# DeltaNet into a gated MLP on one core: the first three fetches of w_in issued from two queues instead of one

## The chip, the cores and the metric

One NeuronCore of a Trainium2 chip runs the whole program. The metric is the device time of one execution in microseconds (us); the time before is the median of 12 runs. The engines are TensorE (PE, with its weight loads PEld), VectorE (DVE), ScalarE (ACT), GpSimd (POOL) and SyncE (SP). SP, ACT and POOL also issue DMAs, each on a queue of its own: q1 is SP's, q10 is ACT's and q0 is POOL's. Sixteen DMA engines carry the packets of all three queues.

## The reference

```python
# attention: batch 4, heads 8, seq 768, head_dim 48, float32
k_n = k / (np.linalg.norm(k, axis=-1, keepdims=True) + 1e-06)
for t in range(S):
    y[:, :, t] = np.einsum('bhd,bhde->bhe', q[:, :, t], state)
    v_old = np.einsum('bhde,bhd->bhe', state, kt)
    state = state + bt[:, :, :, None] * np.einsum('bhd,bhe->bhde', kt, vt - v_old)
# heads joined: x is (3072, 384); w_in is (384, 2048), w_out is (2048, 384), both float64
h = x @ w_in
g = h * (1.0 / (1.0 + np.exp(-1.702 * h)))
return (g @ w_out).astype(np.float32)
```

## The kernel before

**The work.** The sequence is cut into 6 chunks of 128 steps. A unit is one chunk of one batch, so there are 24 units, each with 8 heads. For a unit the kernel normalizes the keys (`normalize_first` for the first seven tiles), transposes them (`transposed`), makes the Gram matrix `G` (`prepare`), sends it through DRAM (`Nd`) to gather the 32x32 diagonal blocks of all heads into `NT`, inverts those blocks on VectorE (`invert`), sends the inverses back through DRAM (`Yd`, then `XB`) and solves the chunk block by block on TensorE (`Step.solve`, `Step.below`) with ScalarE copies (`US`) and VectorE subtractions (`V`) between. The chunk's output goes through the MLP (`hidden`, `written`), whose matmuls fill TensorE for most of the span.

**The weights.** Both weight matrices are float64, and the kernel reads them as raw words. `fetch` brings a part of them into a stage, which lies in a piece of the tile `w_out` that is not yet used. `from_double` turns the two words of each number into float32 with six VectorE instructions (lines 182 to 194), or five and one of ScalarE (line 187) for parts other than the first three. A part of w_in is 128 partitions of 512 numbers. The first three fetches take three parts each (`together_with`): fetch 1 brings parts 0 to 2, fetch 2 parts 3 to 5, fetch 3 parts 6 to 8. Fetch 3 uses the same stage as fetch 1. Later parts are fetched by POOL.

**The four transfers of a fetch.** The rows of w_in are not in the order of the partitions, so a fetch of w_in is four DMAs, listed in `x_rows`: partitions 0 to 47, 48 to 63, 64 to 111 and 112 to 127. For three parts these carry 576, 192, 576 and 192 KB. Every packet is a row of 4096 bytes.

**Order.** The setup at the end of the kernel function issues things in this order: the keys of four units, fetch 1 (`ahead(1, sync)`), the conversion of its parts, the transposes and Gram matrices, the queries and values, more keys (tiles KN4 to KN6), fetches 2 and 3 (`ahead(2, sync)`, line 899), the inversion of the first four units (`invert(0)`), the normalization of KN4 to KN6, and then part 3 (`weights(W1)`). `pinned` operations keep their order in the program; the others are placed by the scheduler, which works from estimated times. The conversion of part 3 and the beginning of part 4 are not pinned. Each engine runs its list strictly in order, its DMA issues included, and a waiting instruction holds all that stand behind it. The line of most helpers is 105, so the names of the tiles tell the operations apart.

Of the kernel before, what the change touches and what calls it, by code (L numbers as in the profile page):

```python
# [18 lines left out]
def kernel(  # L19
# [19 lines left out]
    nc = tc.nc  # L39
# [7 lines left out]
    DP = 64  # L47
# [55 lines left out]
    def pinned(op):  # L103

        return lambda *a, **kw: tc.keep_in_program_order(op(*a, **kw))  # L105
# [106 lines left out]
    def stage(part):  # L212

        if part < parts_in:
            at = part % (2 * KC) * 2 * N_IN
            return at, at + 2 * N_IN
        f = part - parts_in
        if f >= FC - 2:
            return None
        depth = 2 if f < 2 or f >= 8 else 4  # L220
        if f >= 12:
            depth = 1
        at = FC * DM // (2 if f < 2 else 1) - (f % depth + 1) * 2 * DM
        return at, at + 2 * DM

    def together_with(part):

        return list(range(part, part + (KC if part < 3 * KC else 1)))
# [5 lines left out]
    def fetch(part, dma):  # L234

        if part < parts_in:
            j, f0 = part % KC, part // KC * N_IN
            parts = together_with(part)
            shape, src = (len(parts), N_IN), moe_w_in[:, f0 : f0 + N_IN]
            dst = w_in[:, j : j + len(parts), f0 : f0 + N_IN]  # L240
        else:
            parts = [part]
            shape, src = (1, DM), moe_w_out
            dst = target(part)
        if src.dtype != F32:
            if (s := stage(part)) is None:
                raw = wk.tile([128, *shape, 2], I32, tag="xT", name="raw", bufs=3)
            else:
                words = slice(s[0], stage(parts[-1])[1])
                raw = w_out.rearrange("p f d -> p (f d)")[:, words].bitcast(I32)  # L250
                raw = raw.rearrange("p (j n o) -> p j n o", j=shape[0], o=2)
            for i, p in enumerate(parts):
                stages[p] = raw[:, i]
                if s is not None:
                    taken[p] = stage(p)
            dst = raw.bitcast(src.dtype).rearrange("p j n o -> p j (n o)")
        if part < parts_in:
            for p, r, m, step in x_rows:
                row = src[r + j * step : r + j * step + m]
                dma(  # L260
                    out=dst[p : p + m],
                    in_=bass.AP(
                        row.tensor, row.offset, [row.ap[0], [row.ap[0][0] * step, len(parts)], row.ap[1]]
                    ),
                )
        else:
            r = (part - parts_in) * 128
            dma(out=dst if src.dtype == F32 else dst[:, 0], in_=src[r : r + 128, :])
        return parts

    def target(part):
        if part < parts_in:
            j, f0 = part % KC, part // KC * N_IN
            return w_in[:, j, f0 : f0 + N_IN]
        return w_out[:, part - parts_in, :]
# [394 lines left out]
    def ahead(n, dma=nc.gpsimd.dma_start):  # L670

        while n > 0 and waiting and free(waiting[0]):
            staged.extend(fetch(waiting.pop(0), dma))
            n -= 1
# [192 lines left out]
        follow(n)  # L867

    queue = []
    sync = pinned(nc.sync.dma_start)  # L870
    for b in range(0, B, HB):
        normalize_first(b)
    for i in range(B):
# [64 lines left out]
```

## Time and profile before

| | |
|---|---|
| median of 12 runs | 827.59 us (823.05 to 831.54) |
| the profiled execution: time, span | 829.96 us, 828.2 us |
| PE busy in the span | 773.8 us (93%) |
| PE busy from 31 to 57 us / from 220 to 828 us | 9.40 of 26 us / 599.92 of 608 us |
| DVE busy from 31 to 57 us / from 57 to 72 us | 24.48 of 26 us / 14.21 of 15 us |
| mean granted clock of TensorE | 0.946 |
| w_in transfers issued by SP | 6 of 576 KB and 6 of 192 KB |

Times of instructions are counted from the start of the span. A timeline row has the start, the length, the engine, the line, the operation, out<-in with shapes, the count, and in brackets the idle time of the engine before it with what ended that. A "q" behind an engine's name marks its sequencer, which issues DMAs.

### The profile page before, as it was taken

The numbers are of one execution on the slowest core, as the hardware profiler recorded it, in microseconds if no ns is written. First come the engines' busy times: TensorE is split into PE (matmuls) and PEld (weight loads), VectorE is DVE, ScalarE is ACT, GpSimd is POOL, SyncE is SP. The second block draws the span as 40 slices with busy tenths as digits, with TensorE's granted clock in tenths as the row PEclk, the third lists the DMA queues.
The fourth block names the chain that finished last, engine by engine and source line by source line (L and its number), as shares of the span: only waits on it lengthen the run. The fifth ranks groups of instructions, "written<-read, shape, count | busy, mean of one in ns | idle before, by whom it ended". The sixth has DMA issues, their size and how long they took to land.

```text
span 828.2 us, 18734 instructions
## 1 busy us (share of the span) xinstructions
PE 773.8 (93%) x8100; PEld 582.7 (70%) x8100; DVE 485.7 (59%) x1037; ACT 230.3 (28%) x499; POOL 132.0 (16%) x138
## 2 busy tenths in 40 slices
PE   8438798979979999999999999999999999999998
PEld 6327697646866776876867867867867768677684
DVE  6898888687876565675666667667656640100000
ACT  2303542232322332322332322322322323212120
POOL 2113120232021221221222123122201000000000
PEclk9659778987969999999999999999999999999999
DMA  9995732632123323223214204214212010000000
GB/s 146 201 165 138 184 84 66 145 95 76 46 42 81 72 52 78 45 62 85 62 26 101 62 21 101 53 28 94 52 48 56 11 41 11 11 16 1 24 1 19
DMA packets 147314, 55.96 MB, mean 68 GB/s; under 512 B 114336, under 2 KB 143232, under 8 KB 147232
## 3 DMA queue, kind: packets, MB, share of 16 engines
q1 hardware_dynamic: 139488, 41.96, 24.6%
q0 software_dynamic: 2752, 10.62, 4.5%
q10 hardware_dynamic: 4992, 2.20, 1.0%
q8 instruction: 63, 1.03, 0.5%
q14 instruction: 19, 0.16, 0.1%
HBM read 33.13 MB, written 20.45 MB: 65 GB/s over the span
## 4 chain that ended last, share of the span: by engine, by line
PE 75%; DVE 11%; issue 7%; DMA 4%; POOL 1%; ACT 1%; SPq 0%; DVEq 0%; POOLq 0%; ACTq 0%
PE po L105 28%; PE ph L105 25%; PE psY L105 5%; PE psU L105 4%; PE psQ L105 3%; PE ph L638 3%; DVE P L105 2%; PE psG L105 2%; DMA w_out<-in_moe_w_out_dram 2%; DVE YB L105 2%; PE psR L105 2%; PE psT L105 1%; DVE z L105 1%; DMA KN<-in_k_dram 1%; DVE w_in L105 1%
## 5 line engine op out<-in xcount | busy, mean ns | idle before, releaser
L105 PE MATMUL po<-w_out,gT 128*128 128x384 f32 x704 | 239.3, 490 | 0.0
L105 PE MATMUL ph<-xT,w_in 128*128 128x256 f32 x966 | 222.1, 384 | 0.3
L105 PEld LDWEIGHTS ph<-xT,w_in 128*128 128x128 f32 x966 | 180.4, 191 | 30.9 <-issue 2.3
L105 PEld LDWEIGHTS po<-w_out,gT 128*128 128x128 f32 x704 | 130.1, 190 | 82.6 <-issue 1.9
L105 DVE TENSOR_TENSOR V<-V,psR 64x384 f32<-64x384 f32 (+1 forms) x80 | 44.5, 556 | 193.1 <-PE psR L105 192.3
L105 DVE TENSOR_TENSOR P<-NT,YB 64x18 f32<-64x18 f32 (+25 forms) x171 | 82.7, 483 | 4.5
L105 ACT ACTIVATE gT<-ph 128x512 f32<-128x512 f32 x81 | 48.1, 594 | 116.0 <-PE ph L105 115.9
L105 DVE TENSOR_REDUCE YB<-P 64x6 f32<-64x18 f32 (+25 forms) x171 | 72.7, 425 | 5.5
L105 ACT COPY US<-psU 32x384 f32<-32x384 f32 x80 | 37.5, 469 | 123.7 <-PE psR L105 116.9
L105 PEld LDWEIGHTS psU<-V,XB 32*32 32x32 f32 x1280 | 46.0, 106 | 30.2 <-issue 21.2
L533 POOL TENSOR_SCALAR_AFFINE_SELECT M<-M 128x1024 f32<-128x1024 f32 x24 | 29.8, 1243 | 231.6 <-DVE M L105 162.4
L105 PE MATMUL psU<-V,XB 32*32 32x48 f32 x1280 | 54.5, 204 | 4.4 <-DVE V L105 3.9
L638 PE MATMUL ph<-xT,w_in 128*128 128x128 f32 (+1 forms) x282 | 52.1, 345 | 3.1 <-DMA xT<-last 3.1
L105 PE MATMUL psR<-US,G 32*32 32x48 f32 x1920 | 52.8, 203 | 0.3 <-ACT US L105 0.3
L638 PEld LDWEIGHTS ph<-xT,w_in 128*128 128x128 f32 x282 | 44.8, 218 | 7.8 <-issue 4.3
L105 PEld LDWEIGHTS psR<-US,G 32*32 32x32 f32 x1920 | 44.7, 105 | 1.0 <-issue 0.5
L313 POOL TENSOR_TENSOR rn<-ssq,half 128x8 f32<-128x8 f32 x17 | 38.9, 2290 | 2.9 <-DVE ssq L311 2.9
L90 POOL DMA_DIRECT2D KN<-in_k_dram x14 | 13.4, 955 | 154.0 <-PE psY L105 102.1
L154 PE MATMUL ps_warm<-ident 128*128 128x256 bf16 x152 | 21.5, 306 | 16.0 <-DVE ps_warm L105 13.7
L105 ACT COPY o<-po 128x384 f32<-128x384 f32 x22 | 10.5, 478 | 77.7 <-PE po L105 55.8
L105 DVE TENSOR_TENSOR P<-NT 64x256 f32<-64x256 f32 (+7 forms) x36 | 30.6, 849 | 0.3
L154 PEld LDWEIGHTS <-ident 128*128 128x128 bf16 x152 | 16.4, 109 | 19.8 <-issue 13.9
(144 smaller groups left out, 872.6 us busy)
## 6 DMA issues: line engine op xcount, KB each, us to landing
Nd<-G SPq DMA_DIRECT2D x20, 512.0 KB, 3.5
w_out<-in_moe_w_out_dram POOLq DMA_DIRECT2D x14, 384.0 KB, 3.8
QP<-in_q_dram SPq DMA_DIRECT2D x24, 192.0 KB, 3.9
V<-in_v_dram SPq DMA_DIRECT2D x24, 192.0 KB, 3.3
out_dram<-o SPq DMA_DIRECT2D x24, 192.0 KB, 1.9
w_out<-in_moe_w_in_dram SPq DMA_DIRECT2D x6, 576.0 KB, 12.2
NT<-Nd SPq DMA_DIRECT2D x24, 128.0 KB, 2.7
Yd<-YS SPq DMA_DIRECT2D x24, 128.0 KB, 3.2
```

What stands on the lines that cost most here:

```text
L90: dma(out=dst[n % len(dst)][:, :, 0:D], in_=src[b, :, c * C : (c + 1) * C, :].rearrange("h p d -> p h d"),)
L105: return lambda *a, **kw: tc.keep_in_program_order(op(*a, **kw))
L154: pe.matmul(ps, lhsT=ones[:, 0:128], rhs=ones, start=True, stop=True)
L313: nc.gpsimd.tensor_tensor(rn, ssq, half, op=ALU.pow)
L533: nc.gpsimd.affine_select(out=self.M, in_=self.M, compare_op=ALU.is_gt, fill=0.0, base=0, pattern=[[0, H], [1, 128]], channel_multiplier=-1,)
L638: pe.matmul(ph[:, u], lhsT=w_in[:, j, f * 128 : (f + 1) * 128], rhs=xT[:, j, t], start=(j == 0), stop=(j == KC - 1),)
```

## The change

In `fetch`, when the issuing function is SP's pinned one (`sync`), the DMAs for partitions 64 and up go to ACT's queue through a second pinned function (`beside`). This holds for fetches 1, 2 and 3 alike: six of their twelve DMAs move from SP to ACT. Fetches by POOL are not touched, and neither are sizes, stages or conversions.

```diff
         if part < parts_in:
             for p, r, m, step in x_rows:
                 row = src[r + j * step : r + j * step + m]
-                dma(
+                (beside if dma is sync and p >= DP else dma)(
                     out=dst[p : p + m],
...
     queue = []
-    sync = pinned(nc.sync.dma_start)
+    sync, beside = pinned(nc.sync.dma_start), pinned(nc.scalar.dma_start)
```

The built programs differ in three engines' lists; those of PE and POOL are the same. SP loses six DMA issues. ACT gains two of them before the first key transpose's copy, and four between the last of its copies into `M` (line 530) and its copy `NT<-YB` (line 436). On VectorE the conversions of parts 3 and 4 move: in the kernel before they stand in one piece behind the normalization of KN4 to KN6; in the changed one the two line-182 instructions stand inside the inversion, behind its last `TENSOR_REDUCE NT<-P`, two of line 193 among the four pairs of `P<-NT` and `YB<-P` after it, and two each of lines 191, 192 and 194 in the normalization.

## The prediction

> **What bounds the kernel now.** I read the windows by stage first. From 220 us on TensorE is busy 599.92 of 608 us. Before 72 us it is VectorE that works without a break:
>
> ```profile
> core 0: us, PE busy (x) PEld busy (x) DVE busy (x) ACT busy (x) POOL busy (x), PEclk, DMA share, GB/s
> ...
> 31.00:57.00 26.00, 9.40 (x60) 7.59 (x61) 24.48 (x47) 6.26 (x16) 4.36 (x3) 0.50 1.22 168
> 57.00:72.00 15.00, 14.05 (x158) 11.34 (x157) 14.21 (x36) 1.69 (x3) 3.27 (x6) 0.88 0.74 146
> ```
>
> Most of PE's 14.05 us there is `ps_warm` filler, whose result nobody uses. Everything that follows waits for the setup, so a microsecond lost on VectorE before 72 us is a microsecond at the end. The fetches of w_in also stand in this setup. VectorE's timeline shows where they touch it:
>
> ```profile
> 18.67 0.43 DVE L105 TENSOR_SCALAR w_in<-w_out 128x512 int32<-128x512 int32 x1 [1.76 <-DMA w_out<-in_moe_w_in_dram]
> ...
> 29.02 0.69 DVE L105 SCALAR_TENSOR_TENSOR w_in<-tmp,w_in 128x512 f32<-128x512 f32 x1
> 30.76 1.22 DVE L105 TENSOR_TENSOR NT<-NT,bI 128x1024 f32<-128x1024 f32 x1 [1.05 <-DMA NT<-Nd]
> ...
> 50.04 0.42 DVE L105 TENSOR_REDUCE NT<-P 128x64 f32<-128x256 f32 x1
> 50.56 0.42 DVE L105 TENSOR_TENSOR P<-NT 128x256 f32<-128x256 f32 x1
> ...
> 66.01 0.76 DVE L182 TENSOR_SCALAR w_in<-w_out 128x512 int32<-128x512 int32 x2
> ...
> 71.57 1.14 DVE L105 TENSOR_TENSOR V<-V,psR 32x384 f32<-32x384 f32 x2
> ```
>
> Fetch 1 holds VectorE up by 1.76 us, but its conversions end at 29.7 and VectorE then waits 1.05 us more, for `NT`, which comes through ScalarE's copies and DRAM and not from w_in. From 30.76 to 71.57 no idle time is marked. In particular nothing waits for fetch 2: its first conversion, line 182, stands at 66.01. Last, the queues: when they issue, when fetch 2 lands, and at what rate.
>
> ```profile
> 39.20 5.93 SPq L105 DMA_DIRECT2D w_out<-in_moe_w_in_dram  x8
> ```
>
> ```profile
> 43.48 0.65 ACT L530 COPY M<-psQ 128x256 f32<-128x256 f32 x2 [0.21 <-PE psQ L520]
> 44.07 0.64 ACT L436 ACTIVATE NT<-YB 128x256 f32<-128x256 f32 x1
> ```
>
> ```profile
> w_out<-in_moe_w_in_dram SPq DMA_DIRECT2D x1, 192.0 KB, 13.4
> ```
>
> ```profile
> GB/s 163 252 182 144 209 150 135 107 143 150 150 185 228 214 150 107 100 157 164 164 199 214 164 164 107 128 128 157 207 228 185 157 121 114 143 192 264 299 192 50
> ```
>
> The row with 13.4 is fetch 2's fourth transfer: issued at 41.34, landed 13.4 us later, at 54.7. Its second one, issued at 40.39 with 9.3 us, landed at 49.7. So a half (576 + 192 KB, 0.786 MB) takes 5.0 us on one queue, 157 GB/s. The last row is 41 to 64 us in forty slices of 0.575 us. Inside a half the rate sinks to 100 to 128; where one half ends and the next begins, and the 16 engines work on both, it rises to 199 to 228.
>
> **Fetch 1, part by part.** SP loses two issues of 0.31 and 0.43 us behind which it only waits for `Nd`: worth nothing. ACT gets two; their semaphores came at 5.64 us at the latest, and ACT's next work is at 13.53: hidden. If the two halves share the engines well the fetch lands earlier, at best taking away the 1.76 us; the wait for `NT` then grows by as much, so the gain is 0. If it lands later, 1.05 us is covered. One thing is at risk: the keys of the fourth unit, on SP's queue until 8.36 (issued 2.72, 5.64 us), would share the engines with ACT's words. VectorE reads them at 11.71, so 3.3 us cover them; if ACT's half went wholly ahead (5.0 us) 1.7 us would be lost. I take 0, because few key packets are left when ACT's first words can flow.
>
> **Fetch 2, the term that counts.** The program order of the changed kernel puts both line-182 instructions directly behind the reduce of 50.04, so at 50.46 us, and they wait for all four transfers. ACT can issue its two only after its `M` copies: the last of these starts near 43.8, since ACT's list is strict. They then are not alone: SP's queue has gone on to the lower half of fetch 3, so the two queues share the engines, packet by packet. Reckoned from landings: issue 43.8, plus 2.7 us for a short transfer (the page's median of the 128 KB `NT<-Nd`), gives 46.5; then 0.786 MB at half of the joint rate R.
>
> - Lower end of R: one queue's 157 GB/s. 10.0 us, landed at 56.5, a wait of 6.0 us.
> - Upper end: two full queues, 314. 5.0 us, landed at 51.5, a wait of 1.0 us.
> - Taken: 214, the mean of the seven seam slices (209, 228, 214, 199, 214, 207, 228), the only rows in which engines work on different halves. 7.35 us, landed at 53.85, a wait of 3.4 us.
>
> So the words land about when they did before (54.7), but the instruction that wants them has moved from 66.0 to 50.5.
>
> A rule of the Trainium skill speaks against the change: SBUF — State Buffer, section "Can I just issue two DMAs to hit both halves?", says that two concurrent DMAs on tiles at partitions 0 and 64 were measured at only 6% over one, because they serialize on the same engines. The seam slices contradict it in part, since they run 36% over the mean of a half. By the page R would be 166 GB/s, the landing 56.0 and the sum below 5.8 instead of 3.7; I follow the slices.
>
> **What moves on VectorE.** The conversions are the same instructions with the same durations, so `V` at 71.57 comes later by the wait alone. But 0.67 us of line 182 and 1.2 us of line 193 now stand before the memset that releases the 66 `ps_warm` matmuls (57.11 to 66.23). After that filler `psU` comes 1.87 later, at 68.10 instead of 66.74, since 0.51 of it was a wait for `XB`. That is 1.36 us; the first `psR` ended at 69.83 and `V` began at 71.57, so it is covered with 0.4 us to spare. The next filler carries it on: `psU` at 73.04 instead of 72.17, and the second `psR`, which ACT's `US` released at 74.95 while PE was free at 74.38, begins at 75.25. That costs 0.3 us (between 0 and 0.87). `XB` itself lands in time: its transfers come 1.9 us and the wait later, but no longer queue behind fetch 3.
>
> **ScalarE.** Four issues of 0.44 us now stand ahead of `NT<-YB`, which would start near 45.6 instead of 44.07; even at 1.7 us each, the longest issue of these transfers, it ends at 51.3. The reader is the `P<-NT` of 50.56, which itself is held by the wait; without the wait this cover would be 5 us at 0.44 and gone at 1.7. The matmuls' lists and POOL's are unchanged, so what follows shifts as a whole.
>
> **Sum.** 0 (fetch 1) + 3.4 (wait for fetch 2) + 0.3 (filler) = 3.7 us. On the profiled execution, 829.96 us for a span of 828.2, that makes 833.7. This execution is 2.4 us above the median of 827.59, so on the median it is 831.3, 0.45% more. 0.3% is 2.5 us, about what a measurement of this kernel can tell from no change.
>
> **Rivals.**
>
> - *The halves do not mix* (R at 157 to 166). For it: the DMA share is already full. Against it: the seams. Wait 5.5 to 6.0, plus 0.3: 833.4 to 833.9.
> - *The halves do not hinder each other* (R near 314, or ACT's issues start earlier), so not slower. The wait is 0 to 1.0 us and decides from a landing at 51.5 or before: 827.9 to 828.9. For it: at 62 us, when few packets are left, slices reach 264 and 299. Against: no slice between 42 and 60 us passes 228.
> - *The keys are late.* ACT's words overtake the fourth key tile, up to 1.7 us on top: 833.0.
> - *The clock turns it faster.* The granted clock was 0.80 from 72 to 110 us and 0.88 from 110 to 220. Another pattern of load in the setup could raise the second: 100.19 us busy, so 0.03 more is worth 3.4 us, which from about the middle estimate on cancels the wait: 827.9, or 824.5 if the wait is absent too. It could as well fall. No row says which.
>
> **How the numbers follow.** The mixed case gets 0.47, its own range 829.8 to 832.8 (R from 185 to 260). No mixing gets 0.17, no hindrance 0.20, late keys 0.06, the clock 0.10. Slower by over 0.3% (above 830.1): most of the mixed case, no mixing and late keys, 0.62. Faster by over 0.3% (below 825.1): the clock with the wait absent, and what I have not seen, 0.11. Within: 0.27. The range that leaves out 2 in 10 runs from no hindrance, less 1.4 us for the scatter of the runs, to no mixing with 1.6 us of scatter: 826.5 to 835.5.
>
> **What would show it.** Right: VectorE idle by 2 to 5 us before line 182, near 50.5 us, put down to the DMA of w_in; the fourth transfer of fetch 2 landing at 52.5 to 55.5; `V` near 75 us; the wait before the first conversion smaller or gone, that before `NT` larger, and `NT` itself still at 30.8. Wrong: line 182 without a wait, or `NT` not at 30.8. Slices steady at 214 or more over 45 to 58 us show the mixing; 157 shows the rival.

## The result, and the profile after

The changed kernel takes 834.41 us (median of 12 runs, 829.89 to 839.0), the kernel before beside it 826.96 (median of 49). The ratio is 1.0081, with a 95% interval of 1.0059 to 1.0104: by the ratio 6.7 us slower (4.9 to 8.6); the two medians differ by 7.45. The profiled execution took 832.58 us, its span was 830.8 us and its mean granted clock 0.947.

VectorE's timeline of the changed kernel, at the places shown of before:

```profile
19.02 0.43 DVE L105 TENSOR_SCALAR w_in<-w_out 128x512 int32<-128x512 int32 x1 [2.22 <-DMA w_out<-in_moe_w_in_dram]
...
30.88 1.22 DVE L105 TENSOR_TENSOR NT<-NT,bI 128x1024 f32<-128x1024 f32 x1 [0.82 <-DMA NT<-Nd]
...
50.22 0.42 DVE L105 TENSOR_REDUCE NT<-P 128x64 f32<-128x256 f32 x1
60.64 0.76 DVE L182 TENSOR_SCALAR w_in<-w_out 128x512 int32<-128x512 int32 x2 [10.00 <-DMA w_out<-in_moe_w_in_dram]
...
81.32 1.14 DVE L105 TENSOR_TENSOR V<-V,psR 32x384 f32<-32x384 f32 x2 [1.12 <-PE psR L105]
```

Up to the reduce near 50 us none of these rows has moved by more than 0.35 us. Then line 182, which stood at 66.01, is next in the list, and VectorE stands still for 10.00 us until the words of fetch 2 are there. `V` begins 9.75 us later than before. The windows show the same hole: VectorE's 14.21 busy us from 57 to 72 us have become 11.29, and from 31 to 57 us 24.48 have become 18.37.

```profile
31.00:57.00 26.00, 9.41 (x60) 7.59 (x61) 18.37 (x39) 6.33 (x16) 4.13 (x3) 0.50 1.21 170
57.00:72.00 15.00, 3.18 (x16) 2.19 (x16) 11.29 (x19) 1.33 (x2) 0.00 (x0) 0.50 0.41 67
```

The issues: SyncE's four transfers (the lower halves of fetches 2 and 3), then ScalarE's four (the upper halves), in the timelines of their sequencers, and ScalarE's next work.

```profile
39.47 3.32 SPq L105 DMA_DIRECT2D w_out<-in_moe_w_in_dram  x4
```

```profile
43.89 0.34 ACTq L105 DMA_DIRECT2D w_out<-in_moe_w_in_dram  x1
...
44.27 1.42 ACTq L105 DMA_DIRECT2D w_out<-in_moe_w_in_dram  x3
45.81 0.66 ACT L436 ACTIVATE NT<-YB 128x256 f32<-128x256 f32 x1 [1.32 <-DVE P L105]
```

The list of DMA issues has the time to landing; its second row answers to the 13.4 of before.

```profile
w_out<-in_moe_w_in_dram ACTq DMA_DIRECT2D x3, 576.0 KB, 14.5
...
w_out<-in_moe_w_in_dram ACTq DMA_DIRECT2D x3, 192.0 KB, 16.2
```

Both medians are those of fetch 2's upper half, issued at 43.89 and 44.27 us: landed at 58.43 and 60.45. Before, the last of fetch 2 had landed at 54.75.

Why so late is told by the queues of the DMA engines in three windows, each with packets, MB and share of 16 engines: 44 to 50 us, 50 to 53 us, 54 to 62 us.

```profile
q1 hardware_dynamic: 246, 0.87, 104.1%
```

```profile
q1 hardware_dynamic: 98, 0.30, 68.1%
q10 hardware_dynamic: 44, 0.18, 33.3%
```

```profile
q10 hardware_dynamic: 334, 1.15, 97.5%
q1 hardware_dynamic: 2, 0.00, 0.3%
```

In the first window SyncE's queue q1 has the engines for itself, though ScalarE's transfers had been issued before 46 us. Packets of ScalarE's queue q10 begin at 50.6 us, where those of q1 run out, the lower half of fetch 3 included; that half landed at 53.97 and 56.65. The profile does not tell which engine moved a packet: that each engine goes over when it is done with q1 is inferred from the middle window, in which both queues move packets. Nor did the transfer rate rise. The slices of 41 to 64 us, as shown of before:

```profile
GB/s 167 204 202 178 214 207 128 150 135 157 157 135 150 114 142 135 199 135 121 171 185 235 207 164 171 128 164 142 142 157 142 121 178 150 121 107 71 50 7 0
```

All twelve transfers are in at 64.14, against 63.69 before.

### The profile page after: what moved, and what is told of

The parts are those of the page before. It is cut to its first block, busy times and chain, and to the rows that moved or that the text cites. A ratio compares the mean times of both kernels' runs of the same rounds, so it can differ in the third digit from the quotient of the medians.

```text
span 830.8 us, 18734 instructions
## 1 busy us (share of the span) xinstructions
PE 769.4 (93%) x8100; PEld 578.3 (70%) x8100; DVE 484.7 (58%) x1037; ACT 230.7 (28%) x499; POOL 130.8 (16%) x138
## 4 chain that ended last, share of the span: by engine, by line
PE 81%; DMA 6%; issue 6%; DVE 5%; POOL 1%; ACT 1%; SPq 0%; POOLq 0%; DVEq 0%; ACTq 0%
PE po L105 28%; PE ph L105 24%; PE psY L105 5%; PE psU L105 4%; PE psQ L105 3%; DMA w_out<-in_moe_w_in_dram 3%; PE ps_warm L154 2%; PE ph L638 2%; PE psG L105 2%; DMA w_out<-in_moe_w_out_dram 2%; PE psR L105 2%; PE psT L105 1%; PE psG L367 1%; PE po L655 1%; DVE P L105 1%
## 5 line engine op out<-in xcount | busy, mean ns | idle before, releaser
L105 PEld LDWEIGHTS ph<-xT,w_in 128*128 128x128 f32 x966 | 180.0, 190 | 30.7 <-issue 2.3
L638 PE MATMUL ph<-xT,w_in 128*128 128x128 f32 (+1 forms) x282 | 47.7, 325 | 1.0 <-DMA xT<-last 1.0
L638 PEld LDWEIGHTS ph<-xT,w_in 128*128 128x128 f32 x282 | 41.0, 201 | 5.2 <-PE psT L352 1.2
L90 POOL DMA_DIRECT2D KN<-in_k_dram x14 | 13.4, 955 | 152.7 <-PE psY L105 102.1
```

Source lines behind the costliest of these rows:

```text
L90: dma(out=dst[n % len(dst)][:, :, 0:D], in_=src[b, :, c * C : (c + 1) * C, :].rearrange("h p d -> p h d"),)
L638: pe.matmul(ph[:, u], lhsT=w_in[:, j, f * 128 : (f + 1) * 128], rhs=xT[:, j, t], start=(j == 0), stop=(j == KC - 1),)
```

## The experiments

The theory after the result: the loss is one wait, made of a place (the conversion stands near 50 instead of 66 us) and of a landing (60.45 us), and the landing follows from an order of service, in which transfers of two queues are served by time of issue. Rivals: the second queue costs something by itself; SyncE's queue has priority; the queues share the engines, but slowly.

**Late conversions.** The changed kernel with the conversions of parts 3 and 4 held in program order behind the normalization.

```diff
-        if alone:
+        free_ts, free_stt = ts, stt
+        if alone or pin:
             ts, stt = pinned(ts), pinned(stt)
...
+        if pin and not alone and dst.offset != target(NA).offset:
+            ts, stt = free_ts, free_stt
...
-            begun[part] = from_double(dst, stages[part], dst.shape[-1], part < NA)
+            begun[part] = from_double(dst, stages[part], dst.shape[-1], part < NA, part < NA + 2)
```

> The changed kernel with its two queues, but the conversions of fetch 2 are put back behind the normalization, where the kernel before has them (line 182 near 66 us). If the loss is the wait for fetch 2 at its new early place: no wait over 0.5 us before line 182, `V` within 1 us of 71.6, time 826 to 828.5, although fetch 2 still lands at 58 to 60.5. If two queues cost something by themselves (the issues on ScalarE, late keys, the shared engines): 831 to 834.5 in spite of the late conversions.

No wait was left, and `V` began at 71.09, although fetch 2 landed at 59.62. So the wait does come from the place. But the time was 829.83 us, 1.0044 of before (1.0018 to 1.0070), above what the theory allowed. This kernel also differs from before in the order of some instructions, inside these conversions and in many places after 72 us. Two further experiments take that up.

**The early place alone.** The kernel before, all words on SyncE's queue, with the conversions near the places that the changed kernel gives them. The edits of `from_double`, which pin the conversions and move line 193 ahead, are left out here.

```diff
-    run(invert(0))
+    inv = invert(0)
+    ahead_of(inv, 20)
+    begin(NA)
+    begin(NA + 1)
+    ahead_of(inv, 2)
+    next(begun[NA])
+    ahead_of(inv, 1)
+    next(begun[NA + 1])
+    run(inv)
...
```

> The kernel before with all words on SyncE's queue, but the conversions of fetch 2 at the places where the changed kernel has them (the two instructions of line 182 right after the reduce near 50 us). Fetch 2 should land at 54.7 as before. If place and landing explain all: VectorE waits 54.7 - 50.5 = 4.2 us (3.8 to 4.8), `V` near 75.5, time 829.5 to 831.2 (3 to 4 us over the kernel before). If the early place by itself costs as much as the whole change: 833 to 835. If the second queue is what costs: 826.5 to 828.5.

```profile
54.35 0.76 DVE L105 TENSOR_SCALAR w_in<-w_out 128x512 int32<-128x512 int32 x2 [4.05 <-DMA w_out<-in_moe_w_in_dram]
```

This is line 182; where an operation is pinned, the profile has the line of the helper, 105. Fetch 2 landed at 54.16, the wait was 4.05 us and `V` began at 75.55. The time was 830.43 us, 1.0052 (1.0022 to 1.0081). All as expected: the place alone costs 4 us of wait, and the second queue adds the other 6.

**The second queue first.** The changed kernel with the early places written out as above, and SyncE's half of fetch 3 issued behind a transfer of 512 bytes that waits for ScalarE's `M` copies, and so behind ScalarE's half of fetch 2.

```diff
...
-    ahead(2, sync)
+    ahead(1, sync)
+    mark = dram.tile([128, 1], F32, name="mark", tag="mark", bufs=1)
+    sync(out=mark, in_=steps[2].M[:, 7, 0:1])
+    ahead(1, sync)
...
```

> The changed kernel with conversions at the same early places, but SyncE's half of fetch 3 is issued only behind a 512-byte transfer that waits for ScalarE's last `M` copy, so after ScalarE has issued its half of fetch 2. If transfers of the two queues are served in the order of their issue: ScalarE's half lands before SyncE's half of fetch 3, fetch 2 complete at 54.5 to 56, VectorE's wait 4 to 5.5 us, time 829.5 to 831.5. If SyncE's queue has priority over ScalarE's whatever the order: fetch 2 complete at 59 to 61, wait 9 to 10.5, time 833.5 to 835.5. If the two share the engines packet by packet at 157 GB/s in all: complete near 57 to 58.5, wait 6.5 to 8, time 831.5 to 833.

VectorE's timeline, and the queue in the window of 49 to 54 us:

```profile
55.25 0.76 DVE L105 TENSOR_SCALAR w_in<-w_out 128x512 int32<-128x512 int32 x2 [4.80 <-DMA w_out<-in_moe_w_in_dram]
```

```profile
q10 hardware_dynamic: 215, 0.75, 103.3%
```

ScalarE issued at 43.52 and 43.91 and its words landed at 53.65 and 55.06. Its half of fetch 3, issued at 44.45 and 44.92, landed at 61.32 and 61.76. SyncE's half of fetch 3, issued at 46.66 and 48.45, came last, at 62.78 and 63.25. Now it is q10 that has the engines alone. In both kernels the order of landing is the order of issue, so neither queue has priority. Both queues move packets only in the change-overs, of which the second is long (238 packets of q1 and 133 of q10 from 54 to 59 us). The time was 830.10 us, 1.0031 (1.0002 to 1.0060).

**Ten useless microseconds.** The kernel before, conversions late, with idle work on VectorE where the changed kernel waits.

```diff
-    run(invert(0))
+    inv = invert(0)
+    ahead_of(inv, 20)
+    idle = cpool.tile([128, 256], F32, name="idle")
+    pinned(nc.vector.memset)(idle, 1.0)
+    for _ in range(22):
+        pinned(nc.vector.tensor_tensor)(idle, idle, idle, op=ALU.mult)
+    run(inv)
```

> The kernel before, one queue, conversions of fetch 2 late, but VectorE does about 10 us of useless work (a memset and 22 multiplications of 128x256, 0.42 us each, 9.6 us) where the changed kernel waits. No transfer is changed. If a delay of the setup is partly given back by the granted clock later, as the matched instructions of the changed kernel suggest (10 us at 80 to 116 us, 2.6 at the end of the profiled run): `V` later by 9.5 to 10, time later by 6 to 8, like the changed kernel. If the recovery belongs to the two queues (transfers finished earlier, another order): later by 9.5 to 10 at the end too, 836 to 837.5.

`V` began at 81.81, 10.24 us late, and the time was 837.09 us, 1.0130 (1.0089 to 1.0171), that is 10.8 us more (7.4 to 14.1). A microsecond lost on VectorE before `V` is about a microsecond at the end; that the clock gives part of it back is not shown. By the two forecasts above, 837.09 us speaks for the second: what the changed kernel gets back may belong to its queues or its order.

**Two queues against one, in one order.** Both kernels hold all VectorE instructions of these conversions in program order. Every engine runs the same list in both; only the queues of the six transfers differ. Against the kernel before, `V` now stands ahead of the last conversions.

```diff
-        if alone:
+        if alone or pin:
             ts, stt = pinned(ts), pinned(stt)
...
```

> The kernel before with the conversions of fetch 2 held in program order behind the normalization; that puts `V` (71.57) ahead of the last conversions of fetch 2, nothing else moves. It is the partner of the next run: the same order of instructions on every engine, all words on SyncE's queue. `V` should start near 70 (its `psR` ended at 69.83), the conversions be done by 76. Time 825.5 to 828.0, no more than 2 us below the kernel before.

> The same as the run before it, instruction for instruction, but the upper halves of all three fetches on ScalarE's queue. If two queues cost nothing where nobody waits for the words: the time of its partner, within 0.25%. If they cost something by themselves, which the 829.83 us of the two-queue kernel with late conversions could mean: 2 to 4 us more than its partner, with an unchanged `V`, and the clock rows between 72 and 250 us lower.

VectorE's `V`, first with one queue, then with two:

```profile
69.39 1.14 DVE L105 TENSOR_TENSOR V<-V,psR 32x384 f32<-32x384 f32 x2 [0.44 <-PE psR L105]
```

```profile
70.95 1.14 DVE L105 TENSOR_TENSOR V<-V,psR 32x384 f32<-32x384 f32 x2 [2.15 <-PE psR L105]
```

One queue: 825.61 us, 0.9992 of before (0.9968 to 1.0017). Two queues: 825.44 us, 0.9969 (0.9945 to 0.9993), although fetch 2 lands at 60.48. So the second queue costs nothing that these intervals can tell where nobody waits for its words. It gains nothing either.

`V` did begin 1.56 us later with two queues, and the reason shows the order of service once more. `Yd` was issued on SyncE's queue at 57.93 us, just after the last words of that queue had landed (57.74). From 58 to 62 us only ScalarE's queue moved packets, and this `Yd` landed 7.2 us after its issue, at 65.11, behind ScalarE's words (64.85) that had been issued before 46 us; `XB` and `psU` had to wait for it.

```profile
q10 hardware_dynamic: 157, 0.58, 104.1%
```

```profile
Yd<-YS SPq DMA_DIRECT2D x1, 128.0 KB, 7.2
```

Another rival would be that an engine stays with one queue until that queue is empty. The start of the kernel before speaks against it. There SyncE issued the keys and ScalarE the `bI` tiles (beta) in turn, from 0.81 to 2.80 us. In the window of 2.5 to 6 us both queues moved packets, and the last `bI` landed at 7.26, before the last keys at 8.36. So two queues do run side by side where their issues alternate.

```profile
q1 hardware_dynamic: 3079, 0.58, 114.6%
q10 hardware_dynamic: 832, 0.10, 27.7%
```

**Late conversions once more.**

> The two-queue kernel with late conversions once more, to see whether its 829.83 us were chance. The pair with equal orders has shown that the two queues cost nothing by themselves. If this kernel's own order of instructions after 72 us costs (it differs from the kernel before in some places from 72 us on): again 1.003 to 1.006 times the kernel before. If it was chance, or the chip: 0.998 to 1.002.

829.96 us, 1.0026 (0.9994 to 1.0057), between the two ranges that were expected. Together with the first time of 829.83 us, chance is unlikely to be all of it; since no cost of two queues could be told in the pair above, this kernel's order of instructions is left as the suspect. That was not tried by itself.

**Fetch 1 alone on two queues.** The condition of the change, with `and part == 0` added.

> The kernel before, fetch 1 alone split over the two queues; every engine keeps its order of instructions. First conversion at 18.7 to 19.1 us, the wait for `NT` shorter by as much, `NT` at 30.6 to 30.9: time within 1.5 us of the kernel before (825.5 to 828.5). If fetch 1 costs by itself (late keys, late `NT`): `NT` at 31 or later and 828.5 to 830.

First conversion at 18.43, `NT` at 30.49 (both a little earlier than expected), time 826.24 us, 0.9978 (0.9954 to 1.0002). Fetch 1 is worth nothing that can be measured.

**Do mixed halves run faster?** Four kernels on one queue with fetch 2 in small transfers: the first and the last two with the halves alternating, the second with one half after the other. The edit is that of the first.

```diff
+            if part == KC:
+                for i in range(KC):
+                    for p, r, m, step in x_rows[0::2]:
+                        dma(out=dst[p : p + m, i], in_=src[r + i * step : r + i * step + m])
-            for p, r, m, step in x_rows:
+            for p, r, m, step in x_rows[1::2] if part == KC else x_rows:
```

> The kernel before, but fetch 2's words on SyncE's queue in smaller transfers that alternate between the lower and the upper half (six of 48 rows by 512 words, then the two short ones), to have both halves' engines at work at the same time. If mixed halves run at the joint rate the prediction took from the seams: 1.57 MB at 214 GB/s, 7.3 us from first to last landing's end, so fetch 2 complete near 52. If the rate of a half, 157 GB/s, is what the queue gives in any order: complete near 54.5 to 55.5 as before.

> Control for the run with mixed halves: fetch 2 in the same small transfers on SyncE's queue (three of 48 rows by 512 words and the short one, then the same for the upper half), but the halves one after the other. If it was the mixing that brought fetch 2 from 54.75 to 52.2 us: complete at 54 to 55.5, about 157 GB/s. If it was the smaller transfers: complete near 52.

> One queue, fetch 2 in small transfers with the halves alternating, and its conversions at the early places (line 182 right behind the reduce near 50 us). The wait should be landing minus 50.3: fetch 2 complete at 52.2 gives 1.9 us (1.4 to 2.6), against 4.05 with unmixed halves and 10.00 in the changed kernel; `V` near 73.0 to 73.6.

> Candidate for a version better than both: one queue, fetch 2 in small transfers with alternating halves, conversions in program order behind the normalization with `V` ahead of the last of them. Fetch 2 complete near 52.2, fetch 3 near 61; `Yd` no longer behind fetch 3, so `XB` is there before the filler ends and `V` starts at 69.0 to 69.6. Expected 825 to 827, below the kernel before by 0.1 to 0.3%; the mixing itself should add no more than 0.5 us to the 825.6 of the same order without it.

With alternating halves fetch 2 was complete at 52.19, then 53.16 (a wait of 2.88 us and `V` at 74.56, not the 1.9 and 73 to 73.6 expected), then 54.34. With small transfers one half after the other it was 53.86. Five profiled kernels with all of fetch 2 on SyncE's queue in large transfers landed between 53.37 and 54.75. From the landing of the last key tile to the end of fetch 2 the 1.57 MB took 8.51, 9.65 and 8.98 us mixed (185, 163, 175 GB/s), and 10.14, 9.94, 8.91 and 8.88 us unmixed (155, 158, 177, 177: the control, the kernel before, the early place alone, the idle work). In two more unmixed kernels, one queue in program order and fetch 1 alone, it took 10.56 and 10.33 us (149 and 152). On average that is 9.05 us mixed and 9.79 unmixed, and the spread inside each group is wider than this difference: that mixing helps a little is neither shown nor excluded. The first of these runs looked like a proof of 214 GB/s, and the next two took it back.

The last of them is the fastest of the versions that were timed more than once: 822.87 us (825 to 827 expected), 0.9951 (0.9919 to 0.9982). Its `V` began at 70.19, and its order is that of the pair above, whose intervals overlap with its own. Where its gain comes from stays open: the same order on one queue without mixing was 0.9992, and that mixing adds to it is not shown.

## Why the prediction was right or wrong

The sign, the place and the cause, a wait for fetch 2 at line 182, were right, and 834.41 us lies in the range. The size was not: 3.7 us forecast, 6.7 measured. The prediction's own signs missed as well: a wait of 2 to 5 us (10.00), a landing at 52.5 to 55.5 (60.45), `V` near 75 (81.32), and slices at 214 or more from 45 to 58 us (156 on average).

- **Fetch 1: 0.** Right. The wait for its words was 2.22 instead of 1.76 us, the one for `NT` 0.82 instead of 1.05, and `NT` began at 30.88 instead of 30.76. The fourth key tile landed at 8.65 and held nobody up.
- **The wait for fetch 2: 3.4 us, measured 10.00.** This is the step that failed, and not by its rate alone. It let ScalarE's half share the engines "packet by packet" with SyncE's half of fetch 3, from 46.5 us on. In fact the engines finished SyncE's queue first. Reckoned in order of issue, from the landing of the lower half of fetch 2 at 50.58 and with two halves of 5.0 us from the prediction's own row, the words come at 60.6; they came at 60.45. Both ends of the prediction's bounds, 51.5 and 56.5, rested on the same assumption, and so did the rivals on fetch 2. "The halves do not mix" was right about the rate, but still took each queue for half of it. The experiment with the second queue first shows the order of service: the same two queues, issued in the other order, gave a wait of 4.80.
- **The seams.** The 214 GB/s were read as engines working on both halves. One of the seven slices, the 209 from 43.3 to 43.9 us, is no such seam: the last key tile, which landed at 44.81, was still coming in. Kernels that set up the mixing on purpose did not hold 214 (163 to 185).
- **The rule that was weighed.** The 6% of the Trainium skill (SBUF — State Buffer, section "Can I just issue two DMAs to hit both halves?") would have given 166 GB/s and a sum of 5.8 us, nearer to the 6.7 than the slices, but with a wait of 5.5 us still far from the 10.00: it is a rule on rates, and the order of service was missing. In DMA: Bandwidth & Descriptors, section "Queues, rings and completion order", the same skill says that each DMA engine goes round between the queues that have work, a packet at a time. Here the packets did not alternate: q1 moved 246 from 44 to 50 us and q10 none, and from 54 to 62 us it was 2 against 334. Whether the engines themselves kept this order, or ScalarE's packets had not yet reached them, the profile does not show.
- **Filler: 0.3 us, covered at the first `V`.** The delay was sized well: `psU` came 11.43 us late (78.17 after 66.74), 1.43 more than the wait of 10.00, where 1.36 was foreseen. The cover was wrong. From line 182 on VectorE did its work in 1.55 us less than before, probably because conversions now stand between other instructions: in the kernel before, a row that reads what the one ahead of it wrote starts 0.03 us after that one's end (58.17 + 0.55, then 58.75), another 0.08 before it (58.75 + 0.55, then 59.22). So `V` was ready earlier and waited 1.12 us for `psR`. 10.00 - 1.55 + 1.12 us, and 0.18 us of late start, make the 9.75 of `V`. TensorE's timeline of the changed kernel has the filler that was late:

```profile
68.82 7.46 PE L154 MATMUL ps_warm<-ident 128*128 128x256 bf16 x48 [25.01 <-DVE ps_warm L105]
76.12 2.13 PE L105 MATMUL ps_warm<-ident 128*128 128x256 bf16 x18
78.17 0.86 PE L105 MATMUL psU<-V,XB 32*32 32x48 f32 x16
```

- **ScalarE's issues: hidden.** Right: `NT<-YB` began at 45.81, where 45.6 was forecast. Here, too, nothing was won by issuing from a second engine, since ScalarE reached its issues only at 43.89.
- **What follows shifts as a whole.** Not quite. `V` was 9.75 us late, the time 6.7 (4.9 to 8.6). In the profiled executions ScalarE's `G<-psG` at 91.96 came 10.34 us late, its `kT<-psT` at 248.55 only 2.58, and that stayed so to the end. Over the same work, from `V` to that `kT<-psT`, the granted clock was 0.88 (81.32 to 251.13 us), where the kernel before had 0.85 (71.57 to 248.55). That fits the rival in which the clock helps, on top of the wait, but it does not show it. Part of it may be scatter: the profiled execution of the kernel before is 2.4 us above the median of its 12 runs and that of the changed kernel 1.8 below its own. And in the profiled execution with idle work the delay fell too, from 10.26 to 7.42 us between the same two places (clock 0.86), though its runs are 10.8 us longer. Over four kernels with a wait or idle work, `V` was later by 9.75, 3.98, 5.39 and 10.24 us, and the times by 6.7, 4.3, 2.6 and 10.8: 24.4 of 29.4. Each interval is 4 to 7 us wide, so whether a rested TensorE regularly gets a better clock stays open.

So it was luck that the time lies in the range. Two errors of opposite sign met: a wait too short by 6.6 us, and about 3 us of the delay of `V` (9.75 less 6.7) that did not reach the end in this kernel, for a reason that stays open.

## What to carry to other kernels

Here a second DMA queue did not let late words overtake earlier ones: before splitting a transfer, write down the time of issue of everything on both queues, and reckon the landing as if there were one line. Look at what the split does to the order of the consumers: here the harm was a conversion moved up by 15 us to where its words were not yet there, and where it was held back in program order, no cost of the two queues could be told. And test an assumption about sharing with its own rival: bounds on the rate are of no use if the order is wrong.

## What was not expected of the hardware

- Transfers of SyncE's and ScalarE's queues were served in the order of their issue: in the changed kernel words issued at 43.89 landed at 58.43, behind those of the other queue issued at 42.48 (landed at 56.65), and with two queues in program order a `Yd` issued on SyncE's queue at 57.93 landed at 65.11, behind ScalarE's words. Only issues that alternated, at the start, ran side by side.
- Landing times of the same transfers differ from one profiled kernel to the next by more than a microsecond (53.37 to 54.75 us for fetch 2 on one queue).
- One program scatters. The two profiled executions of the kernel with late conversions, on two chips, had spans of 824.6 and 828.5 us. Their matched ScalarE instructions were 0.36 us apart at 91 us and 3.93 us at 248 us, after which the distance stayed; from 110 to 150 us, inside that stretch, the granted clock was 0.96 and 0.91.
